# Two attentions on one core: half a tile of exponentials split between VectorE and GpSimd

## The chip, the cores and the metric

The kernel runs on one core of a Trainium2 chip. The metric is the device time of one execution in microseconds (us). A core has TensorE for matrix products (PE in the profile; PEld is its loading of weights), VectorE (DVE), ScalarE (ACT), GpSimd (POOL) and SyncE (SP), whose queue issues most of the transfers. Each engine works through its own instructions in order; they wait for one another by semaphores. PSUM is the memory into which TensorE writes; GpSimd does not read it in this kernel. SBUF is the main on-chip memory.

## The reference

Two attentions over 2048 tokens of width 576, with 32 heads of 18 columns. Their outputs stand side by side.

```python
# A: full attention; all heads share one k and one v
q = (x @ wq) per head;  k = x @ wk;  v = x @ wv
p = softmax(q k^T * 18 ** -0.5)            # 32 heads x 2048 x 2048
a = (p v of all heads, side by side) @ wo

# B: four segments of 512 tokens, causal inside a segment, with a memory M, z of the segments before
p = softmax(q_s k_s^T * 18 ** -0.5 + mask)
o = g * (phi(q_s) M) / (phi(q_s) z + 1e-6) + (1 - g) * (p v_s)
M, z = M + phi(k_s)^T v_s, z + sum(phi(k_s))
b = o @ wo
```

Everything is float32. Most of the work is A's 134 million exponentials and the two products around them.

## The kernel before, in words

The projections come first (lines 153 to 603): q, k and v go to DRAM, split into two parts each, with an upper bound of every query's scores, which is subtracted inside the score product so that exponentials don't overflow. Then comes the main part, which the change touches.

**Blocks, items and turns.** A's queries are in four chunks of 512; a chunk has eight groups of four heads. One chunk and one group make a *block* of A: 16 tiles of 128 keys (kt), each for two pairs of heads (pr), so 32 *items*. An item is one pair of heads, one key tile and 512 queries. B's 32 blocks of six items each stand between the first blocks of A (the list `after`, line 866). Items are cut into *turns* of three; a block of A has ten turns of three items and one of two. The loop at line 1111 writes out the order of PE, ACT and DVE by hand, turn by turn. In turn k it issues:

- the scores of the turn's items (`scores`, line 906): two matmuls into a buffer E of PSUM, of which there are three, 128 x 1024 numbers. For the middle item of a turn VectorE copies E into SBUF (W, line 934), and ScalarE reads W; for the others ScalarE reads E itself. ScalarE's exponential makes the tile P (line 937), in the order first, third, middle. In B, GpSimd then clears what lies above the diagonal (line 942).
- one step of TensorE's filling (`run_fill`): eight small matmuls of an output projection, into the PSUM bank F; every fifth step VectorE copies F to `osb` (line 794). A projection has 60 steps.
- one slow step, below.
- the products with v of the items of turn k - 2 (`products`, line 950): for each half of the queries four matmuls, one per head, into four stripes of the PSUM tile O. The list `turn_of` says for each pair which key tile it takes at which position m. At a block's end VectorE copies O to `oe` (line 976), which is stored.
- what is due (`due`, line 1014): the steps that finish a chunk or segment. `finish` (line 1028) lays them on later turns: the sums are read back, inverted on VectorE, stored, the heads' tiles `o` and the inverses `rb` are loaded (`load_inverses`, line 740), and GpSimd multiplies them (`weigh`, line 752; here called a *weighing*). A tile of A or of B's first segment takes one weighing and one buffer `rb`, a tile of B's later segments three of each. There are ten buffers `rb`; `room` (line 1058) keeps to them. `due` takes at most two steps a turn and at most two weighings, and none near a block of B.

**The slow tile.** In each block of A the item (kt 0, pr 1) isn't ScalarE's: VectorE computes its exponentials (`exponentials`, line 887). A first step takes the scaled logits out of E (line 892); eight more, one per turn, round off the integer part n, form the remainder, evaluate a polynomial in q, and join it with the exponent. They are 128 x 1024 each. Six have two tensor operands (lines 895, 896, 899 and 902), two a tensor and constants (894, 901). Step 894 comes in the item's own turn, turn 0; the seven others in turns 2 to 8, as turn 1 ends the block before. Its product with v is put off to position m = 12 (`LATE`).

GpSimd's weighings keep the order in which they are written (`keep_in_program_order`).

Of the kernel before, what the change touches and what calls it, by code (L numbers as in the profile page):

```python
# [20 lines left out]
C = 512  # L21
# [28 lines left out]
C5_BITS = 984482944.0  # L50

BY_DVE = ((0, 1),)
LATE = (12,)
QALL = [(slice(0, 36, 2), 0), (slice(1, 36, 2), 1), (slice(36, 54), 0)]
CA = 618
MZ = 126 + 32
# [15 lines left out]
def attention_pair_kernel(ctx, tc, a_xT, a_w, a_wo, b_xT, b_w, b_wo, b_beta, ident_d, hmask_d, bmask_d, cmask_d, sel_d, zmask_d, selx_d, sely_d, out):  # L72
# [667 lines left out]
    def load_inverses(ab, c, t):  # L740

        lo, n, R = H0[t], HT[t], RT[t]
        tiles = [pa.tile([128, C], F32, name="rb", bufs=10)]
        r_d = rA if ab == "A" else rB
        nc.sync.dma_start(tiles[0][:R], r_d[c][lo : lo + n, None, :].to_broadcast([n, DH, C]))
        if ab == "B" and c > 0:
            tiles += [pa.tile([128, C], F32, name="rb", bufs=10) for _ in range(2)]
# [58 lines left out]
    def ask_memory():  # L806

        mz = pa.tile([128, 5, D], F32, name="woA").rearrange("p t d -> p (t d)")[:, : len(LATE_ASK) * 5 * MZ]
        nc.sync.dma_start(mz, mzB.rearrange("p s t m -> p (s t m)"))
        mz = mz.rearrange("p (s t m) -> p s t m", t=5, m=MZ)  # L810
        yield None
        for s in LATE_ASK:
            qf = qfs[s]
            for t in (-1, 0, 1, 2, 3, 4):
                pf = psO.tile([128, C], F32, name="F")
                for hf in range(2):
                    cs = slice(256 * hf, 256 * hf + 256)
                    if t < 0:
                        cols = [(32 * i, i, 126, 32) for i in range(4)]
                    else:  # L820
                        cols = [(32 * j, t, 32 * j, min(32, RT[t] - 32 * j)) for j in range(4) if 32 * j < RT[t]]
                        if t == 4:
                            cols.append((96, 4, 126, 32))
                    for r, i, m, n in cols:
                        R = RT[i]
                        nc.tensor.matmul(pf[r : r + n, cs], mz[:R, s - 1, i, m : m + n], qf[:R, i, cs], start=True, stop=True)  # L826
                    if not hf:
                        yield False
                if t >= 0:
                    R = RT[t]  # L830
                    nc.vector.tensor_scalar(qf[:R, t], pf[:R], gt[:R, t : t + 1], None, op0=ALU.mult)  # L831
                if t < 0 or t == 4:
                    r, n = (0, 128) if t < 0 else (96, 32)
                    dn = pa.tile([128, C], F32, name="rb", bufs=10)
# [12 lines left out]

                at(now[0] + 2, 0, lambda: True, store)
                yield True
# [34 lines left out]

    slow, now = [], [0]

    def exponentials(p, e):

        n = pp.tile([128, 2, 512], F32, name="n", bufs=1)
        q = pp.tile([128, 2, 512], F32, name="q", bufs=1)  # L890
        v = nc.vector
        v.tensor_scalar(p, e, LOG2, -116.0, op0=ALU.mult, op1=ALU.max)
        steps = [
            lambda: v.tensor_scalar(n, p, ROUND, ROUND, op0=ALU.add, op1=ALU.subtract),
            lambda: v.tensor_tensor(p, p, n, op=ALU.subtract),
            lambda: v.scalar_tensor_tensor(q, p, POLY[4], p, op0=ALU.add, op1=ALU.mult),
        ]
        for a in POLY[3:0:-1]:
            steps.append(lambda a=a: v.scalar_tensor_tensor(q, q, a, p, op0=ALU.add, op1=ALU.mult))  # L899
        steps += [  # L900
            lambda: v.tensor_scalar(n.bitcast(I32), n, 2.0 ** 23, C5_BITS, op0=ALU.mult, op1=ALU.add),
            lambda: v.scalar_tensor_tensor(p, q, POLY[0], n, op0=ALU.add, op1=ALU.mult),
        ]
        slow.extend((now[0] + 2 + i, p, step) for i, step in enumerate(steps))

    def scores(it, pr, copied):

        ab, c, hg, kt = it
# [5 lines left out]
        state[it, pr] = p  # L914
        n = 512 if ab == "A" else 512 - 128 * kt if kt < 2 else 384
        if ab == "A":
            for j, r0 in enumerate(HALF):
# [2 lines left out]
            if (kt, pr) in BY_DVE:  # L920
                exponentials(p, e)
                return lambda: None
        else:
            for k, c0 in BKEYS[kt]:
                ks = slice(128 * k, 128 * k + 128)
# [24 lines left out]
    def products(b, m, hf):  # L950
# [5 lines left out]
        o = acc[0]  # L956
        last = (NKT - 1 if ab == "A" else 2) == m
        for j in range(4):
            kt = turn_of[j // 2][m] if ab == "A" else m
            p = state[b + (kt,), j // 2]  # L960
            assert all(x[1] is not p for x in slow)
# [5 lines left out]
            nc.tensor.matmul(  # L967
                o[32 * j : 32 * j + 32, q0 : q0 + n],
                v,
                p[:, j % 2, p0 : p0 + n],  # L970
                start=m == hf == 0,
                stop=last and hf == 1,
            )
# [7 lines left out]


    turn_of = []
    for pr in range(2):
        ks = [kt for kt in range(NKT) if (kt, pr) not in BY_DVE]
        for (kt, p_), pos in zip(BY_DVE, LATE):
            if p_ == pr:
                ks.insert(pos, kt)
# [39 lines left out]
    def finish(k, ab, c, hg):  # L1028
# [58 lines left out]
    with tc.manual_schedule(engines={ENG.PE, ENG.Activation, ENG.DVE}):  # L1087
# [23 lines left out]
        for k in range(len(turns) + 2):  # L1111
# [9 lines left out]
            ends = k > 1 and any(hf and its[n][3] == (NKT - 1 if its[n][0] == "A" else 2) for n, hf in prods[k - 2])  # L1121
            if slow and (slow[0][0] <= k or not ends):
                slow.pop(0)[2]()
            for n, hf in prods[k - 2] if k > 1 else []:
                ab, c = its[n][:2]
                hg = products(its[n][:3], its[n][3], hf)
                if hg in (6, 7):
                    finish(k, ab, c, hg)
                if hg == 7 and ab == "B" and c + 1 < NSEG:
                    load_vseg(c + 1)  # L1130
            due(k)
            if k == len(turns):
                halve_w(0)
            for n, pr in turns[k] if k < len(turns) else []:
# [128 lines left out]
```

## Time and profile before

| | |
|---|---|
| three runs | 1420.92, 1421.37 (median), 1422.42 us |
| the profiled execution | 1422.46 us, of which the profile's span is 1420.8 |
| granted clock of TensorE | 0.998 |
| VectorE, instructions of line 899 | 96, mean 1253 ns |
| VectorE, copies W of line 934, 128 x 1024 | 352, mean 1223 ns |
| GpSimd, clearing in B, line 942 | 192, 94.6 us |
| TensorE's weight loads of line 919 waiting for ScalarE's line 937 | 124.5 us, 348 times |

How to read the rows: a row of a timeline has start and length in us, engine, line, operation, what is written from what, shapes and a count; in brackets the engine's idle time before it and what ended it. Rows next to each other that are alike are merged. A row of groups has the busy time in us and the mean of one in ns behind the bar, then the idle time before them. PE's ends are modelled, so the starts of its weight loads are the better clock.

### The profile page before, as it was taken

What the parts mean: (1) busy time and instruction counts of PE and PEld (TensorE: products, weight loads), DVE (VectorE), ACT (ScalarE), POOL (GpSimd) and SP (SyncE); (2) the same over time, 40 slices, a digit from 0 to 9 for tenths busy, and PEclk for the clock granted to TensorE, in tenths of its full rate; (3) what the DMA queues carried; (4) which work ended last, traced back from release to release, by engine and by line L of the source; (5) the groups of instructions that cost most, each with busy time, mean ns of one, the idle gap of its engine ahead of it and who ended that gap; (6) DMA issues with size and microseconds to landing.
All of it is one profiled execution on the core that took longest, in us unless ns stands there. A gap on an engine that the chain in (4) does not pass through costs nothing.

```text
span 1420.8 us, 40029 instructions
## 1 busy us (share of the span) xinstructions
PE 1404.1 (99%) x17132; PEld 844.8 (59%) x17132; DVE 1034.9 (73%) x1220; ACT 1205.0 (85%) x1448; POOL 248.5 (17%) x326
## 2 busy tenths in 40 slices
PE   9999999999999999999999999999999999999998
PEld 6788888745555555555555555555555555555558
DVE  6656456467787778877777888777778877887773
ACT  4543434479999999999999999999999999999991
POOL 2431000003313214221110160131011400100002
PEclk9999999999999999999999999999999999999999
DMA  9866546467565535332312542232104121110013
GB/s 271 268 207 187 166 144 219 168 175 223 154 212 160 168 117 162 90 113 77 111 58 70 165 131 91 67 107 75 51 34 135 64 75 47 59 44 18 9 60 111
DMA packets 90720, 172.63 MB, mean 122 GB/s; under 512 B 14576, under 2 KB 22889, under 8 KB 90110
## 3 DMA queue, kind: packets, MB, share of 16 engines
q1 hardware_dynamic: 83978, 159.75, 35.9%
q0 software_dynamic: 1664, 4.78, 1.3%
q10 hardware_dynamic: 4896, 5.51, 1.1%
q8 instruction: 135, 2.21, 0.7%
q14 instruction: 47, 0.39, 0.1%
HBM read 99.32 MB, written 70.67 MB: 120 GB/s over the span
## 4 chain that ended last, share of the span: by engine, by line
PE 67%; ACT 9%; issue 2%; DVE 1%; DMA 0%; POOL 0%; ACTq 0%; DVEq 0%
PE O L967 30%; PE E L919 19%; PE F L770 11%; ACT P L937 9%; PE E L928 3%; PE E L1164 2%; PE F L826 1%; DVE W L934 0%; DMA oA<-oe 0%; PE F L1164 0%; PE O L1164 0%; DMA sm<-oA 0%; POOL P L942 0%; DVE osb L794 0%; DVE o L831 0%
## 5 line engine op out<-in xcount | busy, mean ns | idle before, releaser
L937 ACT ACTIVATE P<-E 128x1024 f32<-128x1024 f32 (+1 forms) x800 | 781.7, 1062 | 11.7 <-PE E L919 11.6
L934 DVE COPY W<-E 128x1024 f32<-128x1024 f32 (+1 forms) x384 | 461.0, 1200 | 176.3 <-PE E L919 120.1
L967 PE MATMUL O<-P,VA 128*32 128x256 f32 x7936 | 508.3, 379 | 0.0
L937 ACT ACTIVATE P<-W 128x1024 f32<-128x1024 f32 (+1 forms) x384 | 427.9, 1114 | 3.9 <-DVE W L934 3.7
L967 PEld LDWEIGHTS O<-P,VA 128*32 128x32 f32 x7936 | 262.6, 110 | 146.5 <-issue 5.7
L919 PE MATMUL E<-stA,kstA 56*128 56x512 f32 x1920 | 329.0, 439 | 2.3 <-DVE W L934 1.3
L919 PEld LDWEIGHTS E<-stA,kstA 56*128 56x128 f32 x1920 | 154.9, 184 | 178.1 <-ACT P L937 112.4
L942 POOL TENSOR_SCALAR_AFFINE_SELECT P<-P 128x256 f32<-128x256 f32 (+1 forms) x192 | 94.6, 493 | 474.0 <-ACT P L937 441.5
L758 POOL TENSOR_TENSOR o<-o,rb 126x512 f32<-126x512 f32 (+1 forms) x55 | 81.9, 1504 | 410.2 <-DMA o<-oA 263.8
L770 PE MATMUL F<-woB,o 126*32 126x192 f32 (+1 forms) x1920 | 127.4, 338 | 0.3 <-DVE osb L794 0.3
L899 DVE SCALAR_TENSOR_TENSOR q<-q,PD 128x1024 f32<-128x1024 f32 x96 | 120.3, 1253 | 0.0
L967 PE MATMUL O<-P,vseg 128*32 128x256 f32 (+2 forms) x1536 | 81.8, 344 | 0.4 <-issue 0.3
L770 PEld LDWEIGHTS F<-woB,o 126*32 126x32 f32 (+1 forms) x1920 | 38.2, 108 | 70.7 <-issue 62.7
L976 DVE COPY oe<-O 128x512 f32<-128x512 f32 x64 | 44.2, 691 | 40.7 <-PE O L967 40.0
L249 PE MATMUL pj<-xh,wBl 128*126 128x512 f32 x180 | 72.4, 403 | 0.0
L249 PE MATMUL pj<-xh,wBh 128*126 128x512 f32 x180 | 71.8, 400 | 0.0
L118 ACT CAST qp<-pj 126x512 fp32r<-126x512 f32 (+1 forms) x54 | 30.9, 584 | 44.7 <-DVE kmB L447 32.9
L770 PE MATMUL F<-woA,o 126*32 126x192 f32 (+1 forms) x960 | 63.9, 338 | 0.0
L967 PEld LDWEIGHTS O<-P,vseg 128*32 128x32 f32 x1536 | 49.0, 109 | 24.9 <-issue 2.0
L928 PE MATMUL E<-stB 56*128 56x256 f32 (+3 forms) x512 | 61.2, 347 | 1.3 <-ACT P L937 0.9
L119 DVE TENSOR_TENSOR qp<-pj,qp 126x512 fp32r<-126x512 f32 (+1 forms) x54 | 36.6, 684 | 35.4 <-ACT qp L118 35.2
L249 PE MATMUL pj<-xl,wBh 128*126 128x512 f32 x144 | 57.3, 399 | 0.0
(193 smaller groups left out, 1388.6 us busy)
## 6 DMA issues: line engine op xcount, KB each, us to landing
stB<-kB SPq DMA_DIRECT2D x96, 144.0 KB
stB<-qB SPq DMA_DIRECT2D x32, 288.0 KB
stA<-qA SPq DMA_DIRECT2D x30, 288.0 KB
oA<-oe SPq DMA_DIRECT2D x32, 256.0 KB
oB<-oe SPq DMA_DIRECT2D x32, 256.0 KB
qA<-qp SPq DMA_DIRECT2D x16, 504.0 KB
kB<-qp SPq DMA_DIRECT2D x16, 504.0 KB
qB<-qp SPq DMA_DIRECT2D x16, 504.0 KB
```

The source lines that it names most:

```text
L119: hold(nc.vector.tensor_tensor(qp[:R, 1, :n], src, qp[:R, 0, :n].bitcast(F32), op=ALU.subtract))
L249: nc.tensor.matmul(dst, w[:, c0 : c0 + M], x, start=i == 0, stop=i == len(ops) - 1)
L758: return lambda: tc.keep_in_program_order(nc.gpsimd.tensor_tensor(dst, a, b, op=op))
L770: nc.tensor.matmul(dst[32 * j : 32 * j + 32], parts[ab, c][: RT[t], t, r0 : r0 + 32], wo[ab][: RT[t], t, c0 : c0 + n], start=start, stop=stop,
L899: steps.append(lambda a=a: v.scalar_tensor_tensor(q, q, a, p, op0=ALU.add, op1=ALU.mult))
L919: nc.tensor.matmul(e[:, j], kstA[rows, 128 * kt : 128 * kt + 128], st[rows, h, :], start=True, stop=True)
L928: nc.tensor.matmul(e[:, j, c0 : c0 + 512 - 128 * k], st[rows, 4 + h, ks], st[rows, h, 128 * k :], start=True, stop=True)
L934: nc.vector.tensor_copy(src[:, :, :n], e[:, :, :n])
L937: nc.scalar.activation(p[:, :, :n], src[:, :, :n], AF.Exp, scale=SCALE)
L942: nc.gpsimd.affine_select(diag, diag, pattern=[[0, 2], [0, m], [1, 128]], base=0, channel_multiplier=-1, compare_op=ALU.is_ge, fill=0.0)
L967: nc.tensor.matmul(o[32 * j : 32 * j + 32, q0 : q0 + n], v, p[:, j % 2, p0 : p0 + n], start=m == hf == 0, stop=last and hf == 1,)
L976: nc.vector.tensor_copy(osb, o)
```

## The change

A second piece of the exponentials leaves ScalarE: of the item (kt 2, pr 0) in each block of A, the second of its two heads. This item is the middle one of turn 1, so its E was copied whole to W before. Now VectorE takes the scaled logits of the second head out of E (128 x 512), copies the first head's half to W, and ScalarE does that half alone. The rest of the second head's exponential goes on in turns 2 to 8, one step a turn: VectorE does what has a tensor and constants, and GpSimd the operation on two tensors that follows, where there is one. The fused step of the slow tile, add a constant and multiply by a tensor, is thus two instructions on two engines. The next turn's step reads what GpSimd wrote.

The product with v of this head and key tile moves to position m = 13. As the two heads of a pair now differ, `turn_of` and `state` are kept per head. The three new tiles (nh, qh and PH) take the room of three buffers `rb`: seven are left, and `room` keeps to seven. In a turn with one of these steps `due` lets GpSimd have one weighing, not two. B's second segment has five turns, not six, from the load of the inverses to the weighing.

```diff
-LATE = (12,)
+
+BY_POOL = ((2, 0),)
+
+LATE = ((0, (2, 3), 12), (2, (1,), 13))
...
-        tiles = [pa.tile([128, C], F32, name="rb", bufs=10)]
+        tiles = [pa.tile([128, C], F32, name="rb", bufs=7)]
...
+    def half_exponentials(p, e):
+
+        n = pp.tile([128, 512], F32, name="nh", bufs=1)
+        q = pp.tile([128, 512], F32, name="qh", bufs=1)
+        v, g = nc.vector, nc.gpsimd
+        v.tensor_scalar(p, e, LOG2, -116.0, op0=ALU.mult, op1=ALU.max)
+
+        def behind(dst, a, b, op=ALU.mult):
+            return lambda: tc.keep_in_program_order(g.tensor_tensor(dst, a, b, op=op))
+
+        steps = [
+            (lambda: v.tensor_scalar(n, p, ROUND, ROUND, op0=ALU.add, op1=ALU.subtract), behind(p, p, n, ALU.subtract)),
+            (lambda: v.tensor_scalar(q, p, POLY[4], None, op0=ALU.add), behind(q, q, p)),
+        ]
+        for a in POLY[3:0:-1]:
+            steps.append((lambda a=a: v.tensor_scalar(q, q, a, None, op0=ALU.add), behind(q, q, p)))
+        steps[2:2] = [(lambda: v.tensor_scalar(n.bitcast(I32), n, 2.0 ** 23, C5_BITS, op0=ALU.mult, op1=ALU.add),)]
+        steps.append((lambda: v.tensor_scalar(q, q, POLY[0], None, op0=ALU.add), behind(p, q, n)))
+        apart.extend((now[0] + 1 + i, p, step) for i, step in enumerate(steps))
...
+            if (kt, pr) in BY_POOL:
+                state[it, 2 * pr + 1] = ph = pp.tile([128, 512], F32, name="PH", bufs=1)
+                half_exponentials(ph, e[:, 1])
+                half = pp.tile([128, 2, 512], F32, name="W", bufs=2)
+                nc.vector.tensor_copy(half[:, 0], e[:, 0])
+                return lambda: nc.scalar.activation(p[:, 0], half[:, 0], AF.Exp, scale=SCALE)
...
-        d0, d1, d2, d3 = (0, 2 if hg == 6 else 8, 0, 3) if last else (2, 5, 3, 5) if (ab, c) == ("B", 0) else (2, 5, 3, 6)
+        d0, d1, d2, d3 = (0, 2 if hg == 6 else 8, 0, 3) if last else (2, 5, 3, 5) if ab == "B" and c < 2 else (2, 5, 3, 6)
...
-            return loaded[0] + need <= 10
+            return loaded[0] + need <= 7
...
+            multiplies = apart and apart[0][0] <= k
+            if multiplies:
+                for step in apart.pop(0)[2]:
+                    step()
...
-            due(k)
+
+            due(k, heavy=1 if multiplies else 2)
```

The step's VectorE instruction stands behind the slow step of the same turn, and ahead of the products with v. Left out here are the lines that go from pairs to heads in `products` and `turn_of`.

More of the change, by code (lines that the diff above doesn't have):

```diff
@@ L746, in load_inverses @@
         if ab == "B" and c > 0:
-            tiles += [pa.tile([128, C], F32, name="rb", bufs=10) for _ in range(2)]
+            tiles += [pa.tile([128, C], F32, name="rb", bufs=7) for _ in range(2)]
             nc.sync.dma_start(tiles[1][:R], numB[c][DH * lo : DH * lo + R])
@@ L833, in ask_memory @@
                     r, n = (0, 128) if t < 0 else (96, 32)
-                    dn = pa.tile([128, C], F32, name="rb", bufs=10)
+                    dn = pa.tile([128, C], F32, name="rb", bufs=7)
                     nc.vector.tensor_scalar(dn[r : r + n], pf[r : r + n], 1e-6, None, op0=ALU.add)
@@ L885, in attention_pair_kernel @@
     slow, now = [], [0]
+    apart = []
     def exponentials(p, e):
@@ L913, in scores @@
         p = pp.tile([128, 2, 512], F32, name="PD" if dve else "P", bufs=1 if dve else PBUFS)
-        state[it, pr] = p
+        for j in range(2):
+            state[it, 2 * pr + j] = p[:, j]
         n = 512 if ab == "A" else 512 - 128 * kt if kt < 2 else 384
@@ L958, in products @@
         for j in range(4):
-            kt = turn_of[j // 2][m] if ab == "A" else m
-            p = state[b + (kt,), j // 2]
-            assert all(x[1] is not p for x in slow)
+            kt = turn_of[j][m] if ab == "A" else m
+            p = state[b + (kt,), j]
+            assert (ab, kt) != ("A", 0) or j < 2 or not slow
+            assert (ab, kt, j) != ("A", 2, 1) or not apart
             k, p0, q0, n = (kt, 256 * hf, 256 * hf, 256) if ab == "A" else BHALF[kt][hf]
@@ L969, in products @@
                 v,
-                p[:, j % 2, p0 : p0 + n],
+                p[:, p0 : p0 + n],
                 start=m == hf == 0,
@@ L983, in attention_pair_kernel @@
     turn_of = []
[L984 to L988, printed above, removed]
+    for j in range(4):
+        late = [(kt, pos) for kt, heads, pos in LATE if j in heads]
+        ks = [kt for kt in range(NKT) if kt not in [kt_ for kt_, pos in late]]
+        for kt, pos in late:
+            ks.insert(pos, kt)
         turn_of.append(ks)
```

## The prediction

> **What bounds the kernel now.** I read the page for the shares, then one quiet block of A (nothing on GpSimd) in the windows and each engine's timeline, then the stretches in which GpSimd works, then the tail.
>
> ```profile
> span 1420.8 us, 40029 instructions
> PE 1404.1 (99%) x17132; PEld 844.8 (59%) x17132; DVE 1034.9 (73%) x1220; ACT 1205.0 (85%) x1448; POOL 248.5 (17%) x326
> ```
> ```profile
> 1324.09:1353.08 28.99, 28.99 (x410) 15.17 (x412) 22.68 (x22) 28.75 (x32) 0.00 (x0) 1.00 0.06 21
> ```
>
> The last is a row of the windows: PE, PEld, DVE, ACT and POOL busy. A block of A takes 28.99 us; TensorE and ScalarE both look full in it, VectorE has 6.3 us free, GpSimd is idle. The block has eleven turns, numbered 0 to 10 here: ten of three items and a last of two. TensorE's pitch is seen where the weight loads of a turn's scores begin; under them ScalarE's timeline of the same block:
>
> ```profile
> 1329.26 0.53 PEld L919 LDWEIGHTS E<-stA,kstA 56*128 56x128 f32 x6 [0.41 <-issue]
> ...
> 1331.91 0.53 PEld L919 LDWEIGHTS E<-stA,kstA 56*128 56x128 f32 x6 [0.41 <-issue]
> ...
> 1339.89 0.30 PEld L919 LDWEIGHTS E<-stA,kstA 56*128 56x128 f32 x4 [0.41 <-ACT P L937]
> 1340.47 0.19 PEld L919 LDWEIGHTS E<-stA,kstA 56*128 56x128 f32 x2 [0.29 <-ACT P L937]
> ...
> 1342.65 0.30 PEld L919 LDWEIGHTS E<-stA,kstA 56*128 56x128 f32 x4 [0.41 <-ACT P L937]
> ```
> ```profile
> 1327.37 1.96 ACT L937 ACTIVATE P<-E 128x1024 f32<-128x1024 f32 x2
> 1329.18 1.10 ACT L937 ACTIVATE P<-W 128x1024 f32<-128x1024 f32 x1
> 1330.12 1.97 ACT L937 ACTIVATE P<-E 128x1024 f32<-128x1024 f32 x2
> ...
> 1350.84 1.94 ACT L937 ACTIVATE P<-E 128x1024 f32<-128x1024 f32 x2 [0.24 <-PE E L919]
> ```
>
> TensorE's own turn is 2.65 us (1329.26 to 1331.91), ScalarE's 2.75 (1327.37 to 1330.12: two tiles from PSUM in 1.81, a copied one in 0.94). ScalarE falls back 0.10 us a turn until the scores wait for a buffer E that it hasn't read; then a turn is 2.76 us (1339.89 to 1342.65). In turn 0 it has only two tiles, catches up and even starves (0.24 us at 1350.84). Both are at their limit: some 28.5 us of TensorE's work (ten such turns and a short one), and 0.5 us of waits for a late ScalarE.
>
> VectorE has room in the block, but little in one turn:
>
> ```profile
> 1331.25 1.21 DVE L899 SCALAR_TENSOR_TENSOR q<-q,PD 128x1024 f32<-128x1024 f32 x1
> 1332.75 1.22 DVE L934 COPY W<-E 128x1024 f32<-128x1024 f32 x1 [0.29 <-PE E L919]
> ```
>
> The copy W starts 0.84 us into the turn (1331.91 to 1332.75) and ends at 1333.97; TensorE wants its E back for the second scores of the next turn, two of its six loads, or 0.3 us, into that turn, which begins at 1334.56 (1331.91 + 2.65). So VectorE may run about 0.8 us late before TensorE waits (0.9 less a handover; 0.1 for any handover is an estimate).
>
> **The change, part by part.**
>
> *ScalarE* reads half a copied tile less in turn 1. Activations from SBUF of 1024 and 512 columns:
>
> ```profile
> L937 ACT ACTIVATE P<-W 128x1024 f32<-128x1024 f32 x352 | 397.5, 1129 | 3.9 <-DVE W L934 3.7
> ...
> L386 ACT ACTIVATE ph_e<-ph_e 126x512 f32<-126x512 f32 x28 | 17.7, 632 | 0.7
> ```
>
> That is 0.5 us less ScalarE a block (1129 less 632 ns). Where a block begins starved, as the quiet one does, ScalarE can't use it in turn 1; what goes is one turn of lag, 0.11 us (2.76 less 2.65). Where ScalarE is never ahead, all 0.5 may go. I keep both ends and take a mean of 0.25 for blocks in which nothing else happens.
>
> *VectorE's own steps.* The lengths, from the last blocks' groups and, for 512 columns between SBUF tiles, one cast at the start:
>
> ```profile
> L794 DVE COPY osb<-F 128x192 f32<-128x192 f32 x7 | 2.4, 347 | 0.0
> L976 DVE COPY oe<-O 128x512 f32<-128x512 f32 x3 | 2.1, 692 | 1.9 <-PE O L967 1.9
> ...
> L901 DVE TENSOR_SCALAR n<-n 128x1024 int32<-128x1024 f32 x3 | 2.0, 683 | 0.0
> ```
> ```profile
> 18.21 0.42 DVE L205 CAST xh<-wBl 128x512 fp32r<-128x512 f32 x1
> ```
>
> Turn 1 has a first step and half a copy, both from PSUM, for one whole copy: two of 0.69 for one of 1.22, of which each overlaps its follower by 0.08; about 0.1 us more, in the one turn that has no slow step. I cost it at nothing. Turns 2 to 8 each get one step with a constant: 0.42 us, 0.34 to the next start, seven a block. (683 ns for 1024 columns less a quarter microsecond for half of them gives the same.) Turns 2 to 8 are also those of the slow tile's steps. So VectorE's turn is 1.14 (copy) + 1.13 (slow step, start to start below) + 0.34 = 2.61, and 0.05 for an osb copy (0.35, 0.27 beside its follower) in every fifth: 2.66 against TensorE's 2.65. It fits, with nothing left.
>
> *GpSimd's products* (six a block, 128x512) and the door that they share with VectorE. The nearest rows are the weighings of L758, of the same size; they are also the 70 that stand in the way:
>
> ```profile
> L758 POOL TENSOR_TENSOR o<-o,rb x55: 1274/1291/2305, 428.8 to 1399.5; 126x512 f32<-126x512 f32 x44, 72x512 f32<-72x512 f32 x11
> ...
> L758 POOL TENSOR_TENSOR rb<-rb x15: 1279/2007/2315, 551.6 to 1115.0; 126x512 f32<-126x512 f32 x12, 72x512 f32<-72x512 f32 x3
> ```
> ```profile
> 1097.91 2.53 POOL L758 TENSOR_TENSOR o<-o,rb 126x512 f32<-126x512 f32 x2 [4.61 <-DMA rb<-rB]
> 1100.39 4.54 POOL L758 TENSOR_TENSOR rb<-rb 126x512 f32<-126x512 f32 x2
> ```
> ```profile
> 1099.30 2.21 DVE L899 SCALAR_TENSOR_TENSOR q<-q,PD 128x1024 f32<-128x1024 f32 x1
> 1101.44 1.21 DVE L934 COPY W<-E 128x1024 f32<-128x1024 f32 x1
> 1102.58 1.21 DVE L899 SCALAR_TENSOR_TENSOR q<-q,PD 128x1024 f32<-128x1024 f32 x1
> 1103.71 1.21 DVE L934 COPY W<-E 128x1024 f32<-128x1024 f32 x1
> ```
>
> The columns of the first are shortest, median and longest in ns. A product alone takes 1.28 us. The slow step at 1099.30 took 2.21 for 1.21: it stood behind the product that ended at 1100.44 (1097.91 + 2.53), and its own 1.21 began 0.14 before that. Then GpSimd needed 2.27 for each of two, behind the slow steps. The copies from PSUM took 1.21 throughout. So a product and a two-tensor step of VectorE exclude each other; the copy W goes beside either. The Trainium skill, "SBUF — State Buffer", section "Who interferes with whom", states this exclusion for GpSimd and VectorE's two-input steps, and for single-input steps in a two-port mode as well; by that, the constant steps would be shut out too. The sum below doesn't hang on it, since their data put them into the chain anyway.
>
> In a turn without weighing this does little. The product starts a handover behind its constant step, runs 1.28 beside the next copy W, and holds up the next slow step by 0.18 (0.42 + 0.1 + 1.28 - 0.14, against 0.34 + 1.14). The fourth turn of the seven issues no product. So lag grows by some 0.1 to 0.2 us a turn and falls in turn 7, whose slow step is a short one (0.68): 0.3 us, 0.5 with an osb copy, under the 0.8. Quiet blocks gain.
>
> In a turn with weighing it does not fit. GpSimd's order becomes product, weighing, product; VectorE's next constant step needs the first product, and its step with two tensors falls between. The chain from one constant step to the next is 0.42 + 0.1 + 1.28 (product) + 1.21 (slow step) + 1.28 (weighing), less three overlaps of 0.14: 3.9 us (3.7 to 4.3 with handovers and overlaps at nothing or double), against 2.65 to 2.76. That is 1.15 us too long for each such turn. Before the change GpSimd waited for transfers (4.61 us at 1097.91), not for turns, and took each gap as it came; now the products hold a weighing to its turn. Both orders at the door (VectorE keeping it for two steps, or GpSimd between them) give the same sum.
>
> How many: I followed the kernel's list of due steps through the 416 turns with the new limits (a room of 7, one weighing in a turn with a step, five turns for B's second segment). Of 65 weighings before the end 41 fall into turns 2 to 8, in 13 of the 32 blocks; six of them in turn 8, where no step follows. 35 x 1.15 = 40 us. Off: in 13 blocks the first 0.6 us of lag is free (8 us); six hit the short slow step (3 us); and TensorE's waits for ScalarE in those blocks, up to 0.5 each, are spent already (3 us). Left: 26 us.
>
> *A wait for a transfer.* A weighing that stands at GpSimd for its tile now holds the products behind it, then VectorE's next step, then the copies W, so TensorE and ScalarE.
>
> ```profile
> 432.07 0.53 PEld L919 LDWEIGHTS E<-stA,kstA 56*128 56x128 f32 x6 [0.20 <-issue]
> ```
> ```profile
> 428.79 2.98 POOL L758 TENSOR_TENSOR o<-o,rb 126x512 f32<-126x512 f32 x2
> 438.64 1.66 POOL L758 TENSOR_TENSOR o<-o,rb 126x512 f32<-126x512 f32 x1 [6.88 <-DMA rb<-rB]
> 440.84 3.98 POOL L758 TENSOR_TENSOR o<-o,rb 126x512 f32<-126x512 f32 x2 [0.55 <-DMA rb<-rB]
> ```
>
> These are the weighings of B's first segment, in A's fourth block, whose turn 2 starts at 432.07. The third, put into turn 1, waits for its transfer until 438.64 and ends at 440.30; then comes turn 2's product, to 441.6 or, behind a slow step, 442.7. VectorE's constant step of turn 3 needs it and is due at 437.8 (432.07 + 2.65 + 0.84 + 1.14 + 1.13). 4.3 us less 0.8: 3.5 us, once (0 to 8). For the other segments, whose loads have as many turns, I take nothing (up to this much each).
>
> *Seven buffers.* The weighings of B's last three segments come later (two head tiles at a time, not three), and two output projections start four turns later. That moves four steps of TensorE's filling to the tail, where three stand now in the chain of waits:
>
> ```profile
> 1381.98 1.02 PE F L770 x24
> ```
>
> 1.02 us for three, so 1.4 for four (seven then), less what four emptier turns give back (0 to 1.4): 1 us. The remaining moves, the order of head 1's products and one name per head in the lists, change no instruction's length; its tiles are ready a turn ahead: nothing.
>
> **Sum**, against the profiled execution (1422.46 us, span 1420.8): +26 +3.5 +1, and 19 quiet blocks x 0.25 = -5. That is +25, or 1447.5; the median of the runs is 1.1 us below that execution, so 1446 us.
>
> **The rivals.**
>
> *The weighings find their gaps* (faster). The place is the turn with both; it decides whether such a turn lasts under 2.76 us plus the 0.8. For it: in the rows above GpSimd weighed at 2.27 us apiece, and TensorE lost little. Against: those turns had one product, not two. Then -5 to -8 for ScalarE and +1 for the tail: 1414 to 1418, say 1416.
>
> *VectorE is full in every block.* If a constant step costs 0.2 us more than its row, seven make 1.4 a block on top of the 0.3 to 0.5, past the 0.8; then every block loses about 0.7 and no quiet one gains: 25 + 22 + 5, 1473. For it: 2.66 against 2.65. Against: the lag falls again in turns 7, 9 and 10.
>
> *No product hides at all*: each of five keeps VectorE 1.15 us, a block loses about 4, 1420 + 130, 1550. Against it: the copies' 1.21. The Trainium skill, "Perfetto Trace Analysis", section "Optimizing Scalar/DVE Operations", warns that moving work between these two engines might not help, as they share a port; this would be its full weight, and the trace so far bears out the part with two tensors only.
>
> *Gain and loss cancel*: few collisions, as the weighings bunch in turns 9 to 1: 1419 to 1431.
>
> **How the numbers follow.** About 0.2% (2.8 us) is what a measurement of this kernel can tell. Forecast (1432 to 1462): 0.60. Faster rival: 0.21. Cancelling: 0.09, of which 0.05 lie within 0.2%. Full VectorE: 0.08. None hidden: 0.02. The range leaves out the best of the faster cases and the last two: 1414 to 1464; the forecast's own is 1432 to 1462. Faster 0.21, same 0.05, slower 0.74.
>
> **What would show it.** Right: quiet blocks of A at 28.6 to 28.9 us; blocks with weighings up to 5 us longer; there VectorE idles for GpSimd's products, turns near 3.9; one wait of 3 to 5 us at about 435 us; a tail with seven filling steps instead of three. Wrong: blocks with weighings no longer than the quiet ones (the faster rival), quiet blocks over 29.2 with copies W late in turns 5 to 8 (full VectorE), or constant steps well over 0.42 us.

## The result, and the profile after

The changed kernel takes 1458.62 us (median of 4 runs, 1457.24 to 1459.3) against 1421.14 us before (4 runs, 1420.8 to 1422.42): a ratio of 1.0258, with a 95% interval of 1.0246 to 1.0271. That is 37.5 us more, where the prediction had 25 more. The profiled execution took 1459.3 us. From the page of the changed kernel, the shares and the chain that ended last:

```profile
span 1457.6 us, 40468 instructions
PE 1411.5 (97%) x17132; PEld 847.6 (58%) x17132; DVE 1147.4 (79%) x1476; ACT 1198.6 (82%) x1448; POOL 506.0 (35%) x518
...
PE 56%; DVE 14%; ACT 5%; issue 3%; DMA 1%; SPq 0%; POOL 0%; DVEq 0%; ACTq 0%
PE O L1000 25%; PE E L945 16%; PE F L773 9%; DVE W L966 6%; ACT P L969 5%; PE E L960 3%; DVE qh L926 2%; PE E L1202 2%; DVE q L904 2%; DVE nh L927 1%; DVE qh L928 1%; DVE q L901 1%; DVE sm L729 1%; DMA stB<-qB 0%; DMA sm<-oB 0%
```

ScalarE works 6.4 us less (1205.0 before), as the change meant it to. VectorE, which was 1% of the chain, is now 14% of it: the copies W, constant steps (L926 to L928), the slow steps (L901, L904) and, at 1%, a reciprocal of the sums (L729). The waits say who was held up. In the changed kernel (what waited, for what; us in total, times, longest), and then the two such rows of the kernel before:

```profile
PEld E L945 <- DVE W L966: 41.1, 51, 1.6
...
ACT P L969 <- DVE W L966: 36.5, 44, 1.9
...
PE E L945 <- DVE W L966: 25.6, 34, 1.3
```
```profile
ACT P L937 <- DVE W L934: 3.7, 7, 1.6
PEld E L919 <- DVE W L934: 3.3, 7, 1.6
```

So the loss goes through one wait: the copy W comes late, and TensorE and ScalarE both wait for it. Where, the windows show for three blocks of A (PE, PEld, DVE, ACT and POOL busy): the block with the five weighings of a chunk of A (number 4 of the last chunk), one with a reciprocal of 112x256 sums, and a quiet one.

```profile
1292.98:1325.55 32.57, 30.07 (x412) 15.31 (x408) 29.50 (x31) 29.19 (x32) 17.50 (x11) 1.00 0.16 46
```
```profile
1082.36:1113.19 30.83, 29.12 (x412) 15.33 (x408) 29.06 (x35) 28.13 (x31) 9.00 (x8) 1.00 0.19 61
```
```profile
1354.30:1383.26 28.96, 28.96 (x412) 15.16 (x408) 25.40 (x31) 28.45 (x32) 7.75 (x6) 1.00 0.06 21
```

Before, they took 28.99, 29.07 and 28.99 us. I took the start of each turn's scores from the trace and added up the blocks: the 13 blocks that weigh lost 31.2 us; of the other 19 five that follow a block of B gained 0.39 to 0.43 us each, those after a block of A mostly 0.03 to 0.09, and four that hold a reciprocal, (0,2), (0,5), (1,5) and (2,5), lost 5.0 together. (A pair is chunk and number of the block, both from 0.) The tail after the last turn grew by 2.3 us.

A collision in the first of these blocks, VectorE and then GpSimd:

```profile
1303.42 1.22 DVE L901 SCALAR_TENSOR_TENSOR q<-PD 128x1024 f32<-128x1024 f32 x1
1304.55 1.51 DVE L923 TENSOR_SCALAR qh<-PH 128x512 f32<-128x512 f32 x1
1305.98 1.21 DVE L966 COPY W<-E 128x1024 f32<-128x1024 f32 x1
1307.12 1.38 DVE L904 SCALAR_TENSOR_TENSOR q<-q,PD 128x1024 f32<-128x1024 f32 x1
1308.42 1.50 DVE L927 TENSOR_SCALAR nh<-nh 128x512 int32<-128x512 f32 x1
```
```profile
1302.23 1.29 POOL L919 TENSOR_TENSOR PH<-PH,nh 128x512 f32<-128x512 f32 x1 [11.49 <-PE E L945]
1303.47 2.31 POOL L761 TENSOR_TENSOR o<-o,rb 126x512 f32<-126x512 f32 x1
1306.14 1.28 POOL L919 TENSOR_TENSOR qh<-qh,PH 128x512 f32<-128x512 f32 x1 [0.36 <-DVE qh L923]
1307.38 3.68 POOL L761 TENSOR_TENSOR o<-o,rb 126x512 f32<-126x512 f32 x2
```

Read them side by side. The weighing at 1303.47 finds VectorE's slow step (1303.42 to 1304.64) at the door and takes 2.31 us, 1.02 over its own 1.29. The constant step L923 is next on VectorE, but the weighing has the door: 1.51 us, not the 0.42 of a step that meets nobody. It doesn't wait for data: what it reads, PH, was ready when the product ended at 1303.52. The copy W behind it is 1.1 us late. The next product (1306.14) can't start before that constant step has ended, runs until 1307.42, and costs the next slow step 0.17 (1.38 for 1.21). From constant step to constant step, 1304.55 to 1308.42, are 3.87 us. TensorE's turns under it:

```profile
1306.48 0.18 PEld L945 LDWEIGHTS E<-stA,kstA 56*128 56x128 f32 x2 [0.41 <-issue]
1307.25 0.30 PEld L945 LDWEIGHTS E<-stA,kstA 56*128 56x128 f32 x4 [0.58 <-DVE W L966]
...
1309.67 0.18 PEld L945 LDWEIGHTS E<-stA,kstA 56*128 56x128 f32 x2 [0.41 <-ACT P L969]
1311.12 0.30 PEld L945 LDWEIGHTS E<-stA,kstA 56*128 56x128 f32 x4 [1.26 <-DVE W L966]
...
1313.54 0.68 PEld L945 LDWEIGHTS E<-stA,kstA 56*128 56x128 f32 x6 [0.41 <-ACT P L969]
```

The turns take 3.19 and 3.87 us, and the second scores of each wait for the copy W that gives back their E. The rule of the Trainium skill that the prediction names ("SBUF — State Buffer", "Who interferes with whom") has a second part, that single-input steps in a two-port mode are shut out too; the trace agrees, with 1.51 us for 0.42, though it doesn't show the mode. The same section of the Trainium skill says that whoever issues first has the pair for a whole instruction; these rows agree, as the waiting weighing comes in between two VectorE instructions that follow each other.

### The profile page after: what moved, and what is told of

The parts are those of the page before. It is cut to its first block, busy times and chain, and to the rows that moved or that the text cites. A ratio compares the mean times of both kernels' runs of the same rounds, so it can differ in the third digit from the quotient of the medians.

```text
span 1457.6 us, 40468 instructions
## 1 busy us (share of the span) xinstructions
PE 1411.5 (97%) x17132; PEld 847.6 (58%) x17132; DVE 1147.4 (79%) x1476; ACT 1198.6 (82%) x1448; POOL 506.0 (35%) x518
## 4 chain that ended last, share of the span: by engine, by line
PE 56%; DVE 14%; ACT 5%; issue 3%; DMA 1%; SPq 0%; POOL 0%; DVEq 0%; ACTq 0%
PE O L1000 25%; PE E L945 16%; PE F L773 9%; DVE W L966 6%; ACT P L969 5%; PE E L960 3%; DVE qh L926 2%; PE E L1202 2%; DVE q L904 2%; DVE nh L927 1%; DVE qh L928 1%; DVE q L901 1%; DVE sm L729 1%; DMA stB<-qB 0%; DMA sm<-oB 0%
## 5 line engine op out<-in xcount | busy, mean ns | idle before, releaser
L969 ACT ACTIVATE P<-E 128x1024 f32<-128x1024 f32 (+1 forms) x800 | 771.1, 1036 | 19.6 <-PE E L945 19.5
L966 DVE COPY W<-E 128x1024 f32<-128x1024 f32 (+1 forms) x352 | 419.2, 1192 | 80.4 <-PE E L960 47.6
L969 ACT ACTIVATE P<-W 128x1024 f32<-128x1024 f32 (+1 forms) x352 | 383.2, 1089 | 36.6 <-DVE W L966 36.5
L945 PE MATMUL E<-stA,kstA 56*128 56x512 f32 x1920 | 332.9, 438 | 30.3 <-DVE W L966 25.6
L919 POOL TENSOR_TENSOR qh<-qh,PH 128x512 f32<-128x512 f32 x128 | 164.4, 1285 | 240.4 <-DVE qh L926 197.3
L919 POOL TENSOR_TENSOR PH<-PH,nh 128x512 f32<-128x512 f32 x32 | 41.3, 1290 | 259.3 <-PE E L945 134.8
L904 DVE SCALAR_TENSOR_TENSOR q<-q,PD 128x1024 f32<-128x1024 f32 x96 | 124.6, 1298 | 0.0
L761 POOL TENSOR_TENSOR o<-o,rb 126x512 f32<-126x512 f32 (+1 forms) x55 | 95.1, 1738 | 17.8 <-issue 14.3
```

Of the source, the lines that this page charges most:

```text
L761: return lambda: tc.keep_in_program_order(nc.gpsimd.tensor_tensor(dst, a, b, op=op))
L919: return lambda: tc.keep_in_program_order(g.tensor_tensor(dst, a, b, op=op))
L945: nc.tensor.matmul(e[:, j], kstA[rows, 128 * kt : 128 * kt + 128], st[rows, h, :], start=True, stop=True)
L966: nc.vector.tensor_copy(src[:, :, :n], e[:, :, :n])
L969: nc.scalar.activation(p[:, :, :n], src[:, :, :n], AF.Exp, scale=SCALE)
```

## The experiments

Two theories stood. **The door**: the loss lies in turns that hold a product and a weighing, where constant step, product, slow step and weighing go one after the other. **VectorE is full**: its turn has no room, so any work more, not GpSimd's, makes the copy W late. Reading the blocks had already given the second a place of its own, the reciprocals. Blocks below are counted as above; "the kernel before" has its own runs beside each experiment, and differences are taken from these.

**Seven buffers alone**, without the half tile:

```diff
 (the kernel before)
-name="rb", bufs=10
+name="rb", bufs=7
-            return loaded[0] + need <= 10
+            return loaded[0] + need <= 7
-... (2, 5, 3, 5) if (ab, c) == ("B", 0) else ...
+... (2, 5, 3, 5) if ab == "B" and c < 2 else ...
```

> The kernel before with only the smaller pool: seven inverse buffers, the room bound at seven, and the heads one turn earlier in B's blocks of segments 0 and 1; no half tile. Door theory (the loss sits in turns that hold a GpSimd product and a weighing): this part costs only the four filling steps that move to the tail, 1421 to 1423 us, and the blocks with weighings stay within 1 us of the kernel before. Rival (the weighings, which the smaller pool puts into other turns, are themselves the loss): 1435 us or more, with the 13 blocks that weigh longer by 1 us and more each.

Measured: 1423.16 us against 1421.19 (ratio 1.0014, 1.0005 to 1.0023), just above the door theory's range of 1421 to 1423. The 13 blocks together took 0.4 us more. The last filling in the chain is one row of 40 matmuls, five steps, for 24, three steps, before; the tail grew by 1.4 us.

```profile
1381.24 1.88 PE F L770 x40
```

So the seven buffers cost some 2 us, and moving the weighings costs nothing without the half tile.

**Weighings by VectorE in turns with a half-tile step.**

```diff
-... nc.gpsimd.tensor_tensor(dst, a, b, op=op)
+... (nc.vector if by_vector[0] else nc.gpsimd).tensor_tensor(dst, a, b, op=op)
...
+            by_vector[0] = bool(multiplies)
             due(k, heavy=1 if multiplies else 2)
+            by_vector[0] = False
```

> The changed kernel, but a weighing that falls in a turn with a half-tile step is done by VectorE (about 41 of 65), so that no such turn has two long GpSimd instructions. Door theory (VectorE's constant step waits behind a weighing, product and weighing queue behind each other): the 3.9 us turns go; each such weighing costs VectorE some 0.6 us in its place; 1435 to 1445 us, and the constant step behind the slow step back at 0.4 us. Rival (VectorE is simply full in those blocks): VectorE gets 25 us more work in the same blocks, so the time rises by 5 to 25 us above the changed kernel, 1464 to 1484 us.

Measured: 1443.7 us (1.0163, 1.0147 to 1.0178), in the door theory's range. VectorE's rows by form:

```profile
L927 DVE TENSOR_SCALAR qh<-qh 128x512 f32<-128x512 f32 x96 | 39.8, 414 | 0.0
L761 DVE TENSOR_TENSOR o<-o,rb 126x512 f32<-126x512 f32 x23 | 15.9, 691 | 1.0 <-issue 1.0
```

The constant steps are back at 414 ns, from a mean of 573 in the changed kernel, and 43 weighings (over half of them in the second row) cost VectorE 0.68 to 0.69 us each. The 13 blocks lose 15.6 us in place of 31.2. More work for VectorE, and less time: it isn't the amount of VectorE's work alone. But 15.6 us are left, and all four blocks with a reciprocal lose what they lost.

**The half tile on VectorE alone**: add and multiply in one step, no products on GpSimd.

```diff
-            (lambda: v.tensor_scalar(q, p, POLY[4], None, op0=ALU.add), behind(q, q, p)),
+            (lambda: v.scalar_tensor_tensor(q, p, POLY[4], p, op0=ALU.add, op1=ALU.mult),),
 (the other steps likewise; p - n becomes a second VectorE step)
```

> The changed kernel with the half tile's steps on VectorE alone (add and multiply in one instruction of two tensors), GpSimd has no products left, its weighings alone. Door theory: the weighing blocks lose 1 us or less each instead of 2.4; the quiet blocks lose a little because a turn of VectorE holds 0.3 us more; 1430 to 1445 us. Rival (VectorE is full; GpSimd's products relieve it): 6 steps by 0.3 us in each of 32 blocks are 58 us more VectorE work, 1465 us or more, with the quiet blocks longer by 1 us each.

Measured: 1473.63 us (1.0373, 1.0357 to 1.0389). The rival's number, and my own range missed by 29 us. Two things are in it. The quiet blocks lost 0.2 to 0.6 us each, where the rival had 1: VectorE is full, if by less. But (0,6), (1,6), (2,6) and (3,3), into which the weighings fall when no product holds them to a turn, lost 5.6, 7.0, 6.0 and 4.1. There, VectorE and GpSimd:

```profile
856.15 1.21 DVE L904 SCALAR_TENSOR_TENSOR q<-q,PD 128x1024 f32<-128x1024 f32 x1
857.28 1.78 DVE L923 SCALAR_TENSOR_TENSOR qh<-qh,PH 128x512 f32<-128x512 f32 x1
858.99 1.21 DVE L963 COPY W<-E 128x1024 f32<-128x1024 f32 x1
```
```profile
856.30 3.88 POOL L761 TENSOR_TENSOR o<-o,rb 126x512 f32<-126x512 f32 x2
```

The fused step takes 1.78 us for 0.69: a weighing in between again. The experiment didn't separate the theories, since a fused step has two tensors and meets the same door. What it tells is that the products on GpSimd aren't needed for the collision; a weighing beside a VectorE turn without room is enough.

**The half tile in 12 quiet blocks only.**

```diff
+QUIET = ((0, 4), (1, 2), (1, 3), (1, 4), (2, 1), (2, 3), (2, 4), (3, 1), (3, 2), (3, 3), (3, 5), (3, 6))
-            if (kt, pr) in BY_POOL:
+            if (kt, pr) in BY_POOL and (c, hg) in QUIET:
 (the order of the products with v is chosen block by block as well)
```

> The changed kernel with the half tile only in the 12 blocks of A that hold neither a weighing nor a reciprocal; the other 20 blocks go the old way, with seven buffers throughout. Door theory: no collision is left, and the 12 blocks give what the quiet blocks gave in the changed kernel, 0.03 to 0.4 us each: 2 to 4 us below the kernel before with seven buffers alone, so 1417 to 1421 us. Rival (the half tile costs in every block, the weighings only show it): 12/32 of 37 us, about 1435 us.

Measured: 1420.3 us against 1421.19 (0.9995, 0.9986 to 1.0004): 2.9 us below the kernel with seven buffers alone, as expected. The windows give a block after one of B, (1,2), which took 28.67 us before:

```profile
681.16:709.41 28.25, 28.25 (x412) 15.18 (x409) 25.86 (x31) 27.73 (x31) 8.99 (x8) 1.00 0.43 118
```

The half tile itself is a gain where nothing else stands in its turns.

**No reciprocals**, in the changed kernel and in the kernel before.

```diff
-        nc.vector.reciprocal(sm[:R, :n], sm[:R, :n])
```

> The changed kernel without the reciprocals of the sums (the sums go out as they are, so the output is not normalized). Theory (the reciprocals, 0.9 to 1.8 us of VectorE each in turns 6, 8 and 9, found room in VectorE before and find none beside the half tile): the four quiet blocks that hold one, (0,2), (0,5), (1,5) and (2,5), lose 5.0 us in the changed kernel and would lose none, and the six weighing blocks with one would get some 2 to 6 us back; 1448 to 1453 us. Rival (the reciprocals are not what makes those four blocks longer; the half tile is): 1457 to 1459 us, and the four blocks keep their 0.6 to 2.0 us.

> The kernel before without the reciprocals of the sums. Theory (VectorE had room for them in nearly every block): not over 1.5 us below the kernel before, 1419.5 to 1421.4 us. Rival (they were on the path already, and the changed kernel only shows it): 1415 us or less.

Measured: 1445.66 us (1.0168, 1.0150 to 1.0186) and 1420.13 us (0.9986, 0.9976 to 0.9995), against 1421.53. So the reciprocals, 12.1 us of VectorE's time, cost 1.4 us before and 13.4 us in the changed kernel (37.5 less 24.1). The first is below the range that I expected (1448 to 1453), the second inside its own; the theory holds and its size was too small. The four blocks went from a loss of 5.0 us to a gain of 1.9. What happens, in (2,5) of the changed kernel, on VectorE and under it on TensorE:

```profile
1100.29 1.39 DVE L904 SCALAR_TENSOR_TENSOR q<-q,PD 128x1024 f32<-128x1024 f32 x1
1101.61 0.41 DVE L926 TENSOR_SCALAR qh<-qh 128x512 f32<-128x512 f32 x1
1101.94 1.74 DVE L729 RECIPROCAL sm<-sm 112x256 f32<-112x256 f32 x1
...
1103.92 1.22 DVE L966 COPY W<-E 128x1024 f32<-128x1024 f32 x1
```
```profile
1103.15 0.19 PEld L945 LDWEIGHTS E<-stA,kstA 56*128 56x128 f32 x2 [0.41 <-ACT P L969]
1103.67 0.19 PEld L945 LDWEIGHTS E<-stA,kstA 56*128 56x128 f32 x2 [0.33 <-ACT P L969]
1105.19 0.19 PEld L945 LDWEIGHTS E<-stA,kstA 56*128 56x128 f32 x2 [1.33 <-DVE W L966]
1107.37 0.30 PEld L945 LDWEIGHTS E<-stA,kstA 56*128 56x128 f32 x4 [0.41 <-ACT P L969]
```

No weighing stands in the way here, and the product costs the slow step 0.18 us (1.39 for 1.21). Slow step, constant step and reciprocal fill the turn, the copy W starts at 1103.92, and the turn lasts 4.22 us (1103.15 to 1107.37). In the kernel before, the same reciprocal stands between a slow step and the copy W, with no constant step beside them:

```profile
1075.87 1.75 DVE L726 RECIPROCAL sm<-sm 112x256 f32<-112x256 f32 x1
1077.65 0.29 DVE L729 TENSOR_SCALAR sm<-sm,omg 112x128 f32<-112x128 f32 x1
1077.85 1.22 DVE L934 COPY W<-E 128x1024 f32<-128x1024 f32 x1
```

and its turn lasted 3.02 us, for 2.78 in the kernel before without reciprocals.

**Short weighings**, with and without the reciprocals: VectorE's instructions as in the changed kernel, GpSimd's weighings on 64 columns.

```diff
-... nc.gpsimd.tensor_tensor(dst, a, b, op=op)
+... nc.gpsimd.tensor_tensor(dst[:, :64], a[:, :64], b[:, :64], op=op)
```

> The changed kernel with every weighing cut to 64 of its 512 columns (the other columns are left as they are, so the output is not normalized); VectorE's instructions are the same. Door theory (GpSimd's weighing of 1.28 us stands between VectorE's slow step and its constant step, and ahead of the product): the 3.9 us turns go back below 2.9 us and the 13 blocks lose under 8 us in place of 31; 1432 to 1437 us, what is left being the reciprocals and the tail. Rival (VectorE's own work fills those turns): no more than a few us gained, 1452 us or more.

> The changed kernel with both: weighings of 64 columns and no reciprocals. If collisions with weighings and the reciprocals in full VectorE turns are the whole loss, all 32 blocks are as quiet as the 12 of the quiet-only kernel: 1418 to 1424 us (seven buffers' 2 us and the first blocks' 2 us against 3 to 5 us of gain). Rival (something else of the half tile costs as well): 1427 us or more, and its place is seen block by block.

Measured: 1427.43 us (1.0038, 1.0025 to 1.0050) and 1418.6 us (0.9977, 0.9967 to 0.9986). With short weighings the 13 blocks lose nothing (-0.2 us together), at the same work for VectorE: the rival is out for them. The block that took 32.57 us in the changed kernel, number 4 of the last chunk, with short weighings:

```profile
1264.99:1293.97 28.98, 28.98 (x413) 15.25 (x409) 25.66 (x31) 28.47 (x32) 12.73 (x11) 1.00 0.18 51
```

The first result is 5 us below the range that I expected, the second inside it. With both, no block after the first three is longer than before by more than 0.5 us, and the kernel is 2.9 us below the kernel before, 1.5 below the kernel before without reciprocals. The loss is closed: weighings 31.6 us (37.5 less 5.9), reciprocals 8.8 more (5.9 and 2.9), rest -2.9. With the weighings whole, the reciprocals cost 13.4, so 4.6 of it is there only beside whole weighings. By the blocks of the four profiles, 3.3 of that lies in the 13 that weigh, and some 1.6 of this in a stretch of half clock in one of them (see the open points); how much dearer a reciprocal and a weighing make each other isn't settled.

**How many collisions.** The kernel without reciprocals and with short weighings, of which the first one, or the first two, in turns 2 to 7 of a block are whole.

```diff
+                w = C if whole() else 64
+                tc.keep_in_program_order(nc.gpsimd.tensor_tensor(dst[:, :w], a[:, :w], b[:, :w], op=op))
 (whole: in turns 2 to 7 of a block of A, the first one, or the first two)
```

> The changed kernel without reciprocals and with weighings of 64 columns, but the first weighing that falls into turns 2 to 7 of a block of A has all its 512 columns (13 in all, one in each of the 13 blocks). The prediction's step (the first 0.6 us of lag in a block is free): at most 0.55 us in each, 0 to 4 us above the kernel with short weighings only, 1419 to 1422 us. Rival (no lag is free, since it is paid back in the short turn 10 and the next block's turn 0): the full price of one collision, 0.7 to 1.15 us in each of the 13, 1427 to 1433 us.

> The same with the first two weighings whole in each block (up to 24). The prediction's step: the second costs its full 1.15 us, so 10 to 14 us above the kernel with one whole weighing, and 1431 to 1435 us. Rival (every collision costs alike): 11 more collisions cost 0.7 to 1.15 us each, 8 to 13 us, as the 13 before: 1436 to 1444 us.

Measured: 1427.31 us (1.0042, 1.0029 to 1.0054) and 1436.23 us (1.0104, 1.0088 to 1.0119), against 1421.74. The trace has 12 and 22 whole weighings there, not 13 and 24. The first dozen cost 8.5 us, 0.7 each, the next ten 8.9, 0.9 each; by the blocks 0.5 to 1.0, and 0.94 to 1.0 in nine of ten. The rival is nearer: some 0.2 us of the first lag is free, not 0.6. TensorE's turns in (3,4) with one, and with two:

```profile
1276.34 0.18 PEld L962 LDWEIGHTS E<-stA,kstA 56*128 56x128 f32 x2 [0.41 <-issue]
...
1279.54 0.19 PEld L962 LDWEIGHTS E<-stA,kstA 56*128 56x128 f32 x2 [0.41 <-ACT P L986]
...
1282.44 0.68 PEld L962 LDWEIGHTS E<-stA,kstA 56*128 56x128 f32 x6 [0.41 <-ACT P L986]
```
```profile
1285.17 0.19 PEld L962 LDWEIGHTS E<-stA,kstA 56*128 56x128 f32 x2 [0.41 <-issue]
...
1288.36 0.19 PEld L962 LDWEIGHTS E<-stA,kstA 56*128 56x128 f32 x2 [0.41 <-ACT P L986]
...
1292.23 0.68 PEld L962 LDWEIGHTS E<-stA,kstA 56*128 56x128 f32 x6 [0.41 <-ACT P L986]
```

One collision makes the two turns behind it 3.20 and 2.90 us (0.80 over 2.65 twice); with a second, the 2.90 becomes 3.87.

**A version to keep.** The quiet-only kernel, with the room for an inverse given back after each weighing step, and the same without a half tile.

```diff
-            tiles += [pa.tile([128, C], F32, name="rb", bufs=7) for _ in range(2)]
+            tiles += [pa.tile([128, C], F32, name="rb", bufs=7) for _ in range(2)][::-1]
...
             box[t, t].pop(0)()
+            loaded[0] -= 1
             if box[t, t]:
 ...
-            loaded[0] -= need
```

> The quiet-only kernel, with the room for inverses given back tile by tile (one after each weighing step) and not only after the last of three, so that seven buffers start the output projections as early as ten did. Theory (seven buffers cost through four filling steps in the tail, and the half tile in 12 quiet blocks gains 2 to 3 us): 1 to 2 us below the quiet-only kernel, 1418 to 1420 us, and so below the kernel before by 0.1 to 0.2%. Rival (the loads now wait for their tile on SyncE's queue, or the seven buffers cost elsewhere): 1420 us or more.

> Its control without any half tile: the kernel before with seven buffers, given back tile by tile. Theory: the same time as the kernel before with ten, 1420.5 to 1422 us. Rival (seven buffers cost elsewhere than in the tail): 1422 to 1423.5 us, as with seven buffers alone.

Measured: 1420.13 us (0.9989, 0.9980 to 0.9998) and 1422.34 us (1.0008, 0.9998 to 1.0017), against 1421.21. The tail is back at the length of before in both (44.6 us, and 46.1 with seven buffers alone). Yet both came out in the ranges of their rivals, the control above the one that I expected, and the intervals of the kernels with and without the early release overlap: its gain of 1 to 2 us is not shown, nor that seven buffers cost through the tail alone. The half tile in 12 blocks is worth 2.2 us in this pair and 2.9 in the pair before. The first of the two is, by its median, the fastest kernel here that leaves no work out, 1.1 us below the kernel before, which is less than the 0.2% that can be told with confidence.

## Why the prediction was right in sign and 12 us short, point by point

- **What bounds the kernel, and through which wait** (VectorE late, TensorE waiting for its E, ScalarE for its W): right, by the rows of waits.
- **ScalarE's gain** (0.25 us in each of 19 quiet blocks, -5): right in size where a block is quiet. 12 blocks gave 2.2 to 2.9 us, 0.2 each, and unevenly: 0.4 behind a block of B, where ScalarE is the later engine (in (1,2) three turns went from 2.77 to 2.65 us), and next to nothing elsewhere. Of the other seven, four hold a reciprocal; two are the first blocks, which lost 1.7 us together and 1.8 without reciprocals and with short weighings. In the first of them the granted clock was 0.5 for 6.8 us, for 3.4 in the kernel before; in two kernels without a half tile there that had 6.8 us too (seven buffers alone, quiet-only) it lost 0.8 and 1.0, so most of its loss isn't the half tile's. What the second loses its 0.4 to stays open. The seventh is the last block, whose length goes with a transfer of its sums.
- **VectorE's turn, "It fits, with nothing left"**: this is the step that failed. 2.66 against 2.65 is right for a turn with a copy, a slow step, a constant step and a fifth of an osb copy; but I summed one quiet block's instructions and let the reciprocals out, the longer of which take 0.94 and 1.74 us each, eight in all. A sum that ends with nothing left has to name all that VectorE does in any block. The runs put 13.4 us on it beside 27.0 for the collisions, or 8.8 beside 31.6, as the 4.6 that they share are counted: most of the 12.5 us that the prediction lacked.
- **Product and two-tensor step exclude each other; quiet blocks hide it**: right. No product in any block took over 1.30 us: they never waited at the door, the weighings and VectorE did.
- **The chain of 3.9 us**: right as a sum, 3.87 in the rows, but with a wrong link. The prediction let each constant step wait for the product that it reads, and said that the sum doesn't hang on whether constant steps are shut out. Groups of them in the changed kernel:

```profile
L926 DVE TENSOR_SCALAR qh<-qh 128x512 f32<-128x512 f32 x96 | 55.0, 573 | 0.0
L928 DVE TENSOR_SCALAR qh<-qh 128x512 f32<-128x512 f32 x32 | 19.9, 621 | 0.3 <-POOL qh L919 0.3
```

  The 0.3 us is all that constant steps sat idle for products in the whole kernel. What held them was the weighing at the door: 33 of the 224 took over 1.2 us, and with short weighings 0.55 was the longest. If it didn't, the constant step would run beside the weighing, and product, slow step and weighing alone would repeat every 3.4 us (an estimate that no run tests: 1.28 + 1.21 + 1.28 less three overlaps of 0.14). So "VectorE idles for GpSimd's products" didn't come, and constant steps well over 0.42 us, which the prediction gave as a sign of being wrong, did.
- **Its price**: 35 collisions at 1.15 less 14 us of rebates were 26; the runs give 27.0 (without reciprocals) to 31.6. The sum held, its parts didn't: a collision costs 0.9 and not 1.15, and of the "first 0.6 us of lag" only some 0.2 are free. In the changed kernel 37 weighings stand between the first and the last product of a block, of which 26 took over 2.2 us. That price and rebate, both too large, offset each other is luck. The lag that I called free is probably paid back when the copy W of a late turn meets the short turn 10 and the next block's turn 0; no run separates this.
- **A wait for a transfer in A's fourth block (+3.5)**: wrong. GpSimd there, in the changed kernel:

```profile
433.11 2.98 POOL L761 TENSOR_TENSOR o<-o,rb 126x512 f32<-126x512 f32 x2
441.51 1.28 POOL L919 TENSOR_TENSOR PH<-PH,nh 128x512 f32<-128x512 f32 x1 [5.42 <-DVE nh L922]
442.74 2.26 POOL L761 TENSOR_TENSOR o<-o,rb 126x512 f32<-126x512 f32 x1
```

  The third weighing stands behind the first product, not ahead of it, and that waits for VectorE (nh at 441.0, behind two steps of B's memory, lines 834 and 838, of 0.74 and 0.70 us). So the 5.42 us in the row, near the place where the prediction had a wait of 3 to 5, are no wait for a transfer. The block lost 2.4 us, and two collisions cost 1.9 of it in the kernel with two whole weighings.
- **Seven buffers (+1)**: right in kind: behind the last products stand seven filling steps for three (56 weight loads for 24), as forecast, and this is 1.4 us in the tail, some 2 us in the time. The changed kernel has eight there (64), and its tail is 0.9 us longer still; the quiet-only kernel, with seven buffers and no half tile in the last block, has seven.
- **Rivals.** "The weighings find their gaps" fell with the first collision. "VectorE is full in every block" is wrong for the changed kernel (twelve quiet blocks gain), and right for the half tile on VectorE alone, which by chance also has its 1473 us.

Open: the last block of A differs by some 3 us between kernels that are alike in it. VectorE waits there for the sums (1.8 us in the profile of the kernel before, 2.2 in the control's), and in the control's the granted clock was 0.5 for 3.4 us of it. So this much of any difference of two profiles, 1.4 us of it in the changed kernel's favour, is no effect of the change. And turn 0 of (3,0) took 5.74 us in the changed kernel's profile, against 2.67 without reciprocals; 1.75 of it is a wait for ScalarE behind a late W, and 1.7 are pauses of TensorE (0.81 and four of 0.21) in a stretch, 1174.4 to 1177.8 us, in which the granted clock was 0.5. Turns 0 and 1 of (2,0), with the same wait and a full clock, took 1.6 us less. Why the clock fell in the one and not in the other the traces don't show.

## What to carry to other kernels

When new steps bring an engine's turn to the length of the bounding engine's, list every instruction that this engine issues in any turn, the rare ones above all: the reciprocals that cost 1.4 us in all while VectorE had room cost 13 when it had none. And an engine that ran ahead of the turns (GpSimd's weighings before) can lose that freedom when something on its queue waits for each turn; put the new work where its queue and the partner's are empty, here in 12 blocks of 32, and the small gain stays.

## What the runs showed of the hardware that was not expected

A constant step of 512 columns, 0.41 us alone, takes 1.50 behind a weighing, a GpSimd instruction of two tensors, though it reads only one tensor; copies from PSUM took 1.21 beside both. A GpSimd instruction that waits for a VectorE step gets in before the VectorE instruction that follows at once, in both collisions shown above. And a weighing cut to an eighth of its columns isn't an eighth of the time: on average 693 ns, with 317 for the shortest and 1387 for the longest, as some wait for a slow step.

```profile
L761 POOL TENSOR_TENSOR o<-o,rb 126x64 f32<-126x64 f32 x44 | 30.0, 693 | 19.1 <-issue 14.4 <-DMA o<-oA 4.2
```
